# One order of steps for another in a kernel of gated attention and a feed-forward layer

## The chip, the cores and the metric

The kernel runs on one core of one Trainium2 chip. A core has five engines with a queue of instructions each: PE (TensorE, matrix products), ACT (ScalarE), DVE (VectorE), POOL (GpSimd) and SP (SyncE, which here issues nearly all DMA). The engines run beside each other and meet at semaphores. PE writes its products into PSUM, which has 8 banks; ACT and DVE read them from there. The metric is the time of one execution on the device in microseconds (us), lower is better; the median of three runs before the change is 181.44 us (180.72 to 181.81).

## The reference

Attention with a gated state runs over 4 batches, 8 heads, 768 positions and 48 numbers for each head; its output goes through a feed-forward layer with 384 inputs and 2048 inner units.

```python
f = 1.0 / (1.0 + np.exp(-f_logit))
for t in range(S):
    state = f[:, :, t, :, None] * state + np.einsum('bhd,bhe->bhde', k[:, :, t], v[:, :, t])
    y[:, :, t] = np.einsum('bhd,bhde->bhe', q[:, :, t], state)
x = y.transpose(0, 2, 1, 3).reshape(B * S, H * D)     # 3072 x 384
h = x @ w_in                                          # w_in 384 x 2048
g = h * np.cos(h)
out = g @ w_out                                       # w_out 2048 x 384
```

All inputs and the output are float32.

## The kernel before

The 3072 rows are cut into twelve pairs of 256 positions; pairs 0 to 2 belong to the first batch, and so on, and each pair needs the state that the pair before it in its batch left. The feed-forward layer works in twelve units of 256 rows, one for each pair. The function `describe` builds some 950 named steps, `pair(n)` those of attention and `moe(m, ...)` those of the layer. In a name, the first number is the pair, unit or row block, what follows the point is a part of it.

The steps of a pair are these, with the line of `kernel.py` on which the profile shows them:

- `f`, `k`, `q`, `v` load the inputs (L296); pairs 0 and 1 load f, k and q in halves of four heads.
- `ex`, `ln`, `fx`, `fy` on ACT make the logarithm of the gate, the gate and a factor (L329, L333, L347, L344); `ad` on POOL adds two logarithms (L363); `cum` on PE sums them over 64 positions (L374, L380); `eb` and `ei` on ACT turn the sums into decay factors (L391, L395).
- `qa` and `ka` lead q and k on (L338 or L341, and L351), `qm` and `km` multiply them with the decay factors (L404).
- `tq` and `tk` transpose the results, for pairs 0 to 3 on PE (L435, then `qkt` copies them out of PSUM), for pairs 4 to 11 `tq` is a DMA that SP issues (L424).
- `sc` on PE makes the scores (L455), `am` on DVE masks them (L459).
- `vb` and `vt` copy v into two layouts (L197, a helper for all copies).
- `ps` on PE makes the new part of the state (L477), `st` and `sz` on DVE add the old state and decay it (L495, L501).
- `y` and `yi` on PE give the output of attention (both L529), `xe` copies it out of PSUM (L197).

The steps of a unit are `h` (products with w_in, L577), `co` (a sine on ACT that gives the cosine, L582), `g` (the product h cos h on DVE, L559), `o` (products with w_out, L593), `ot` (copy out of PSUM, L197) and `out` (the store, L604). `w0`, `w1` load the two weight matrices in four parts each (L282) and `wc0`, `wc1` cast them to bfloat16 (L197). `zf` is a product of zeros into an unused bank (L264), `z...` with a tile's name sets a buffer to zero (L231).

Nothing in this program chooses the order at run time. The string `ORDER` lists all steps as `name:engine` with the letters T (PE), S (ACT), V (DVE), G (POOL), Y (SP), and with the number of the buffer or PSUM bank that a step's result gets. `emit` goes through it and issues each step on its engine, so that the string fixes the order of every queue; a buffer that is given out again makes the new writer wait for the last readers:

```python
    for word in ORDER.split():
        name, how = word.split(":")
        plan.append((G.steps[name], LETTER[how[0]], [int(x) for x in how[1:].split(",") if x]))
```

`SLOTS` says how many buffers there are of a kind (3 each for f, k, q, v, 5 for g, which weights on their way in use too). When ACT passes from the functions of the gate to the sine or back, it loads a table; both orders do so ten times.

Of the kernel before, what the change touches and what calls it, by code (L numbers as in the profile page):

```python
# [48 lines left out]
ei3:S1 k1.1:Y ka1.1:G ln2:S0 fy2:S km1.1:V ps1.0:T7,0 ad2:G1 vt1.1:G tq1.1:T6 zf43:T1 zf44:T1  # L49
zf45:T1 zf46:T1 tk1.1:T qkt1.1:S0 sz0.10:V qkt1.0:V2 ps1.1:T zf47:T1 sc1.0:T4 st1.00:V st1.01:V  # L50
xe0.1:S0 am1.0:V2 fx3:S cum2:T1 eb2:S2 xe0.0:V fx2:S ei2:S2 w0.0:Y1 wc0.0:G zf48:T6 zf49:T6 zf50:T6
zf51:T6 sc1.1:T4 am1.1:V0 h0.01:T2 h0.00:T sz1.00:V0 y1:T6,1 co0.0:S2 sz1.01:V st1.11:V yi1:T
xe1.0:S1 st1.10:V w0.1:Y0 wc0.1:G xe1.1:V sz1.10:V0 h0.11:T4 k3:Y2 ka3:G h0.10:T h1.01:T6 sz1.11:V
co0.1:S0 g0.0:V0 h1.00:T km3.1:G0 tk3.1:T0 co1.0:S3 g0.1:V q3:Y0 qa3:G qm3.1:G tq3.1:T qm3.0:G
h1.10:T2 km3.0:G w0.2:Y1 wc0.2:S w0.3:Y2 wc0.3:G h1.11:T co1.1:S1 qkt3.1:V3 sc3.1:T4 g1.0:V3
h1.20:T0 h1.21:T co1.2:S0 h0.31:T6 h0.30:T co0.3:S2 am3.1:V3 q2:Y1 qa2:G qm2.0:G2 w1.2:Y4 wc1.2:G
k2:Y2 h0.21:T4 g1.1:V h0.20:T co0.2:S3 tq3.0:T2 tk3.0:T g1.2:V g0.3:V h1.31:T0 h1.30:T co1.3:S1
tq2.0:T3 g0.2:V o3.2:T6 o2.2:T7 o0.2:T4 qm2.1:G ka2:G km2.0:G km2.1:G o1.2:T5 tk2.0:T qkt3.0:V1
w1.3:Y1 wc1.3:S g1.3:V o2.3:T o3.3:T sc3.0:T0 am3.0:V1 qkt2.0:S4 sc2.0:T2 am2.0:V2 w1.0:Y2 wc1.0:G
# [18 lines left out]
co4.3:S0 st6.10:V g4.3:V h4.21:T0 h4.20:T co4.2:S2 o6.0:T ot6:S3 h5.11:T2 h5.10:T co5.1:S3 h4.10:T4
g4.2:V st6.11:V sz6.11:V2 g5.1:V3 h4.11:T co4.1:S2 g4.1:V h5.20:T0 h5.21:T o9.3:T7 co5.2:S1 g5.2:V
sz6.10:V o9.0:T o8.0:T2 o8.3:T vb7:G0 qa6:G qm6.0:G qm6.1:G f8:Y1 tq6.1:Y4 sc6.1:T4 am6.1:V2  # L80
tq6.0:Y3 sc6.0:T0 ka7:G km7.0:G1 vt7.2:G2 vt6.0:G0 km7.1:G vt6.1:G qa7:G qm7.0:G vt7.0:G ps7.1:T6,3
ps7.0:T vt6.2:G vt7.1:G st7.00:V sz7.00:V1 st7.01:V sz7.01:V st7.11:V st7.10:V sz7.10:V0 v8:Y1
out2:Y out6:Y sz7.11:V out4:Y q9:Y1 tq7.0:Y2 ex9:S ln9:S1 ex8:S vt6.3:S qm7.1:G tq7.1:Y0 o8.2:T
o9.2:T o8.1:T ot8:V1 o7.1:T4 o9.1:T o7.3:T fy9:S ad9:G2 cum9:T5 ln8:S0 fy8:S am6.0:V0 o7.0:T o7.2:T
ot7:V0 ad8:G1 vt7.3:G cum8:T6 yi6:T3 qa9:G ot9:V3 fx9:S y6:T2 xe6.1:V1 fx8:S ei9:S2 eb9:S2 vb8:G0
k9:Y0 ka9:G km9.0:G2 q8:Y0 qa8:G vt8.2:G0 f10:Y0 k8:Y2 q10:Y2 sc7.0:T0 am7.0:V3 f11:Y2 out5:Y out8:Y
sc7.1:T4 am7.1:V1 eb8:S1 ei8:S1 v9:Y0 ka8:G km8.0:G0 vt8.1:G h5.00:T6 xe6.0:S qm8.0:G tq8.0:Y1
km9.1:G qm9.1:G vb9:G1 qm9.0:G km8.1:G h5.30:T2 h5.31:T co5.3:S3 g5.3:V h6.30:T0 h5.01:T co5.0:S0
g5.0:V h6.31:T out7:Y v10:Y1 out9:Y tq9.0:Y3 tq9.1:Y4 yi7:T4,5 y7:T xe7.1:V3 xe7.0:S co6.3:S3
g6.3:V1 h6.20:T2 h6.21:T co6.2:S2 g6.2:V h6.01:T6 h6.00:T co6.0:S1 h6.11:T4 h6.10:T co6.1:S0  # L90
h7.11:T0 h7.10:T h7.20:T2 h7.21:T g6.0:V o12.0:T7 g6.1:V o10.2:T5 o12.3:T co7.1:S3 o13.0:T6 g7.1:V0
co7.2:S2 g7.2:V sc8.0:T0 vt9.2:G1 qm8.1:G tq8.1:Y0 ps8.1:T4 ps9.0:T2,3 vt9.1:G ps9.1:T sz9.00:V1
ps8.0:T st8.00:V sz9.01:V st8.01:V sz8.01:V3 st9.11:V o13.2:T o10.1:T sz8.00:V o12.1:T st9.10:V
o13.3:T sz9.10:V2 ex11:S ln11:S1 ad11:G1 ex10:S vt9.3:G sz9.11:V ln10:S0 fx10:S cum11:T2 o12.2:T
ei11:S0 eb11:S1 o13.1:T ad10:G0 cum10:T3 vt9.0:S ot13:S2 ei10:S2 o11.1:T4 o11.0:T ot12:V1 am8.0:V3
# [620 lines left out]
```

## Time and profile before

| what | number |
|---|---|
| median of 3 runs | 181.44 us (180.72 to 181.81) |
| span of the profiled execution, first to last instruction | 178.2 us |
| what lies around the span, against that median | 3.2 us |
| PE busy, fill products among it | 170.5 us |
| DVE busy | 136.6 us |
| ACT busy | 127.2 us |
| POOL busy | 112.9 us |
| read from and written to memory | 25.17 MB and 4.72 MB |

The profile comes from one execution; no time of its own is listed for it beside its span. Times in its rows are counted from the start of the span. A row of a group gives the line, the engine, the operation, what it writes and reads, how often; behind the first bar the busy time in all and the mean of one in nanoseconds, behind the second the idle time of the engine just before these instructions and who ended it. A row of the timeline begins with start and length in microseconds. A row of the chain has start, length and what the last-ending chain of work did there.

### The profile page before, as it was taken

What the parts mean: (1) busy time and instruction counts of PE and PEld (TensorE: products, weight loads), DVE (VectorE), ACT (ScalarE), POOL (GpSimd) and SP (SyncE); (2) the same over time, 40 slices, a digit from 0 to 9 for tenths busy, and PEclk for the clock granted to TensorE, in tenths of its full rate; (3) what the DMA queues carried; (4) which work ended last, traced back from release to release, by engine and by line L of the source; (5) the groups of instructions that cost most, each with busy time, mean ns of one, the idle gap of its engine ahead of it and who ended that gap; (6) DMA issues with size and microseconds to landing.
All of it is one profiled execution on the core that took longest, in us unless ns stands there. A gap on an engine that the chain in (4) does not pass through costs nothing.

```text
span 178.2 us, 5848 instructions
## 1 busy us (share of the span) xinstructions
PE 170.5 (96%) x2475; PEld 122.8 (69%) x2478; DVE 136.6 (77%) x206; ACT 127.2 (71%) x179; POOL 112.9 (63%) x145
## 2 busy tenths in 40 slices
...
GB/s 148 261 261 264 307 221 362 328 359 277 293 258 258 222 241 232 289 166 188 246 198 274 255 198 238 178 287 143 2 59 169 144 48 4 0 88 4 0 177 88
DMA packets 74394, 34.46 MB, mean 193 GB/s; under 512 B 67456, under 2 KB 72832, under 8 KB 74368
## 3 DMA queue, kind: packets, MB, share of 16 engines
...
q8 instruction: 19, 0.31, 0.7%
...
HBM read 25.17 MB, written 4.72 MB: 168 GB/s over the span
## 4 chain that ended last, share of the span: by engine, by line
PE 84%; DVE 6%; SPq 4%; DMA 3%; issue 1%; ACT 1%; DVEq 0%
PE ps L593 36%; PE ps L577 35%; PE ps L529 5%; SPq L296 4%; PE ps L455 3%; DMA k<-in_k_dram 3%; DVE am L459 2%; PE ps L477 2%; DVE qk L404 1%; PE ps L435 1%; PE ps L374 1%; DVE ps L495 1%; ACT w_in_bf L197 1%; DVE x L197 1%; PE ps L264 0%
## 5 line engine op out<-in xcount | busy, mean ns | idle before, releaser
L559 DVE TENSOR_TENSOR g<-ps,co 128x1024 bf16<-128x1024 f32 x48 | 58.0, 1222 | 20.0 <-ACT co L582 17.1
L582 ACT ACTIVATE co<-ps,halfpi 128x1024 bf16<-128x1024 f32 x48 | 53.0, 1114 | 24.5 <-PE ps L577 21.4
L593 PE MATMUL ps<-w_out_bf,g 128*128 128x384 bf16 x384 | 68.0, 326 | 0.0
L577 PE MATMUL ps<-x,w_in_bf 128*128 128x256 bf16 x576 | 66.9, 273 | 0.4 <-ACT w_in_bf L197 0.3
L577 PEld LDWEIGHTS <-w_in_bf 128*128 128x128 bf16 x576 | 55.5, 98 | 9.0 <-ACT w_in_bf L197 0.5
L593 PEld LDWEIGHTS <-g 128*128 128x128 bf16 x384 | 36.2, 98 | 21.5
L459 DVE TENSOR_TENSOR am<-ps,pmask 128x1024 bf16<-128x1024 f32 x24 | 28.8, 1219 | 4.3 <-PE ps L455 4.0
L197 POOL COPY vt<-vb 64x384 bf16<-64x384 bf16 x40 | 20.6, 516 | 3.1 <-ACT vb L197 1.3
L404 POOL TENSOR_TENSOR qk<-q,b 128x384 bf16<-128x384 f32 x21 | 20.9, 1002 | 2.0 <-DVE q L338 1.3
L404 POOL TENSOR_TENSOR qk<-k,bi 128x384 bf16<-128x384 f32 x20 | 19.9, 1001 | 0.7
L264 PE MATMUL ps<-zero 128*128 128x512 bf16 x49 | 14.8, 426 | 1.5 <-DVE zero L203 1.2
L501 DVE TENSOR_TENSOR sz<-ps,b 64x192 bf16<-64x192 f32 x40 | 14.1, 352 | 2.4 <-PE ps L477 1.6
L351 POOL TENSOR_TENSOR k<-k,f 128x384 f32<-128x384 f32 (+1 forms) x13 | 11.8, 909 | 6.0 <-DMA k<-in_k_dram 3.5
L197 ACT COPY ot<-ps 128x384 f32<-128x384 f32 (+1 forms) x15 | 6.6, 456 | 9.6 <-PE ps L593 5.0
L495 DVE TENSOR_TENSOR ps<-ps,sz 64x192 f32<-64x192 f32 x32 | 11.7, 365 | 1.8 <-PE ps L477 0.8
L329 ACT ACTIVATE f<-f 128x768 f32<-128x768 f32 (+1 forms) x14 | 10.4, 744 | 3.3 <-DMA f<-in_f_logit_dram 2.6
L363 POOL TENSOR_TENSOR sp<-ls 128x384 bf16<-128x384 f32 x10 | 10.1, 1007 | 4.0 <-ACT ls L333 3.8
L341 POOL TENSOR_TENSOR q<-f,q 128x384 f32<-128x384 f32 x10 | 10.0, 998 | 3.9 <-ACT f L344 2.8
L197 POOL CAST vb<-v 128x768 bf16<-128x768 f32 x10 | 8.6, 856 | 1.5 <-DMA v<-in_v_dram 1.5
L455 PEld LDWEIGHTS <-qkt 48*64 48x64 bf16 x384 | 6.2, 106 | 4.5 <-issue 2.4
L455 PE MATMUL ps<-qkt 48*64 48x128 bf16 x384 | 8.8, 220 | 0.5 <-DVE am L459 0.2
L264 PEld LDWEIGHTS <-zero 128*128 128x128 bf16 x52 | 4.8, 105 | 5.7 <-issue 1.9
...
## 6 DMA issues: line engine op xcount, KB each, us to landing
...
```

The lines of the kernel that those rows point to most:

```text
L197: (nc.scalar.copy if e == "ACT" else eng(e).tensor_copy)(out=o, in_=i)
L264: G.step(f"zf{i}", ("PE",), lambda e, dump=dump: nc.tensor.matmul(dump.ap, lhsT=zero[:, 0:128], rhs=zero, start=True, stop=True), writes=[ ...
L351: eng(e).tensor_mul(out=w.ap[:, :, 0, :], in0=w.ap[:, :, 0, :], in1=t.ap[:, :, 0, :])
L404: G.step(f"{nm}{n}.{u}", ("POOL", "DVE") if cut else ("POOL",), lambda e, u=u, j=j, src=src, dec=dec: eng(e).tensor_mul(out=qkp[u][j].ap[: ...
L455: nc.tensor.matmul(o[64 * h:64 * h + 64, r, 2 * a + g, :].rearrange("p (e n) -> p e n", e=2), lhsT=qkv(u)[s, 1, a, g, h, :], rhs=qkv(u)[s, ...
L459: G.step(f"am{n}.{u}", ("DVE",), lambda e, u=u, sc=sc: nc.vector.tensor_mul(out=am[u].ap.rearrange("p r b n -> p (r b) n"), in0=sc.ap.rear ...
L495: nc.vector.tensor_add(out=view()[s], in0=view()[s], in1=S0.ap[s, :, r, :])
L501: eng(e).tensor_mul(out=new.ap[s, :, r, :].rearrange("p (u a) n -> p u a n", u=2), in0=view()[s].rearrange("p (u a) n -> p u a n", u=2), i ...
L559: nc.vector.tensor_mul(out=o.rearrange("p b (n e) -> p b n e", e=2), in0=ph.ap.rearrange("p (b e n) -> p b n e", e=2, n=64), in1=co.ap.rea ...
L577: nc.tensor.matmul(ph.ap[:, i * T:(i + 1) * T].rearrange("p (g t) -> p g t", t=C), lhsT=w_in_bf[:, kk, f0:f0 + 128], rhs=xa[:, :, kk, :], ...
L582: G.step(f"co{m}.{j}", ("ACT",), lambda e, ph=ph, co=co: nc.scalar.activation(out=co.ap, in_=ph.ap, func=AF.Sin, bias=halfpi), reads=[ph], ...
L593: nc.tensor.matmul(po.ap[:, 0:DM], lhsT=gT.ap[:, j, i * C:(i + 1) * C], rhs=w_out_bf[:, j, :], start=(po.first and j == 4 * s), stop=(po.f ...
```

## The change

`ORDER` is replaced as a whole: 928 steps instead of 947. The work is the same except for 19 of the 52 fill products, which are gone. The order of every queue is new, and so are most buffers and banks. Among the loads, `v0` comes second and `k0`, `q0` before `f1`; `f6` and `v6` come behind the DMA transposes of pairs 4 and 5, where they were ahead of them. Some steps change engine: `km0.0`, `km0.1` and `km1.1` go from DVE to POOL, `qm0.1` from DVE to POOL and `qm1.1` from POOL to DVE, twelve more of the 48 `vt` copies from POOL to ACT (20 instead of 8), three casts of w_out instead of one and no cast of w_in on ACT (`wc0.2` on POOL), `vb2` and `vb3` from ACT to POOL and `vb10` the other way, `qkt0.0` to DVE and `qkt3.1` to ACT, eleven `ot` (`ot23.0` among them, to ACT) and seven `xe` one way or the other between ACT and DVE, `ka0.1` to DVE. On PE the products with the weights stand between clusters of attention's short products in both orders, in other places.

```diff
--- before.py
+++ after.py
...
 WITHIN = 12
-ZEROS = 52
+ZEROS = 33
...
 ORDER = """
-f0.1:Y0 zqk.1:G zsp.1:G zvt.0:G zsz.0:V zsp.2:V zsp.0:V zqk.0:G zvt.2:G zsz.3:G f0.0:S zsz.2:V
-ex0.1:S ln0.1:S1 fx0.1:S zf0:T0 zf1:T0 zf2:T0 zf3:T0 zf4:T0 zf5:T0 zf6:T0 zf7:T0 zf8:T0 cum0.1:T7
-ei0.1:S2 ex0.0:S f1.1:Y1 k0.1:Y0 ln0.0:S fx0.0:S ex1.1:S zf9:T6 zf10:T6 zf11:T6 zf12:T6 cum0.0:T0
-ka0.1:G km0.1:V1 zvt.1:V zf13:T1 tk0.1:T3 v0:Y2 ei0.0:S eb0.0:S2 q0.1:Y0 eb0.1:S qa0.1:V qm0.1:V
-zf14:T2 zf15:T2 zf16:T2 zf17:T2 zf18:T2 zf19:T2 zf20:T2 zf21:T2 tq0.1:T vb0:G1 k0.0:Y ka0.0:G
-vt0.1:G1 zsz.1:G vt0.2:G km0.0:V zf22:T2 zf23:T2 zf24:T2 zf25:T2 zf26:T2 tk0.0:T4 qkt0.1:V1 zqk.2:V
-f1.0:Y ex1.0:S ln1.0:S1 ln1.1:S fx1.1:S ps0.0:T2,5 ps0.1:T sz0.00:V1 f3:Y2 ex3:S q0.0:Y qa0.0:V
-fx1.0:S sz0.01:V vt0.3:G ln3:S1 ad3:G0 k1.0:Y2 ka1.0:V cum1.1:T1 ei1.1:S0 v1:Y1 st0.11:V qm0.0:V
-eb1.1:S0 fy3:S st0.10:V vb1:G0 vt1.2:G0 cum1.0:T7 ei1.0:S sz0.11:V3 zf27:T6 zf28:T6 zf29:T6 sc0.1:T2
-am0.1:V3 q1.1:Y1 qa1.1:V qm1.1:G0 zf30:T6 zf31:T6 zf32:T6 zf33:T6 tq0.0:T qkt0.0:S4 zf34:T6 cum3:T6
-zf35:T0 zf36:T0 sc0.0:T0 vt1.3:S f2:Y0 km1.0:V zf37:T4 zf38:T4 zf39:T4 tk1.0:T4 am0.0:V1 q1.0:Y
-eb3:S1 vt0.0:S zf40:T2 zf41:T2 zf42:T2 y0:T2,3 yi0:T qa1.0:V eb1.0:S qm1.0:V tq1.0:T vt1.0:G ex2:S
...
-vt3.0:G vt2.3:G k5:Y0 f6:Y1 v4:Y2 ps3.0:T1,2 ps3.1:T sz3.00:V2 ps2.0:T3 ps2.1:T vt2.1:G o0.0:T
-st2.00:V sz3.01:V q5:Y0 v5:Y1 o1.3:T o1.0:T ad4:G0 sz2.00:V1 st3.10:V sz3.10:V3 sc2.1:T0 ad5:G2
-st2.01:V sz2.01:V am2.1:V0 o2.1:T o3.1:T fx5:S ot2:V1 ot3:V0 st3.11:V o0.1:T qa4:G yi2:T0,3 y2:T
-xe2.0:V1 xe2.1:V yi3:T1 y3:T7 cum4:T6 ei4:S1 ka4:G sz3.11:V eb4:S0 qm4.1:G0 o1.1:T ot1:V2 ot0:V3
-km4.0:G qm4.0:G v6:Y0 tq4.0:Y3 ka5:G km4.1:G tq4.1:Y2 cum5:T0 eb5:S2 ei5:S0 xe3.0:V3 h2.11:T2
-h2.10:T co2.1:S0 vb4:G2 xe3.1:V h2.20:T4 g2.1:V1 h2.01:T6 h2.00:T co2.0:S2 g2.0:V f7:Y0 vt4.2:G0
-fy5:S out1:Y out3:Y vt4.0:G qa5:G qm5.0:G1 km5.0:G tq5.0:Y1 km5.1:G qm5.1:G tq5.1:Y0 vb5:G0 h3.10:T0
...
-y4:T6,0 yi4:T xe4.0:V2 ps5.1:T1 ps5.0:T st5.00:V sc5.1:T4 am5.1:V2 fx7:S vt5.0:G vb6:G1 vt5.2:G
-vt5.1:G ka6:G sc5.0:T2 am5.0:V0 cum7:T6 o6.1:T o6.2:T xe4.1:S h4.01:T4 eb7:S0 ei7:S0 h4.00:T
-co4.0:S0 h3.01:T2 st5.01:V sz5.01:V2 y5:T0,6 sz5.00:V yi5:T xe5.1:S0 fy6:S g4.0:V0 h3.00:T xe5.0:V
...
-o21.3:T ot21:S2 o22.1:T4 o22.3:T ot20:S1 out20:Y out16:Y g11.2:V o22.2:T g11.0:V o22.0:T ot22.1:S1
-out22.1:S o23.0:T7 o23.1:T ot22.0:V o23.3:T o23.2:T ot23.0:V3 out22.0:S ot23.1:S out14:Y out21:Y
-out23.1:Y out23.0:S
+zsp.1:G zvt.0:G f0.0:S2 f0.1:Y ex0.0:S ln0.0:S1 zvt.2:G v0:Y0 ex0.1:S ln0.1:S zf0:T7 zf1:T7 zf2:T7
+zf3:T7 zf4:T7 zf5:T7 zf6:T7 zf7:T7 zf8:T7 cum0.0:T0 zqk.0:V zsz.0:V fx0.0:S zvt.1:V ei0.0:S1 vb0:G1
+vt0.2:S1 k0.0:Y1 ka0.0:G k0.1:Y fx0.1:S q0.0:Y1 qa0.0:V q0.1:Y f1.0:Y0 km0.0:G0 zf9:T7 zf10:T7
+cum0.1:T3 eb0.1:S2 ei0.1:S f1.1:Y ka0.1:V eb0.0:S qm0.0:V ex1.0:S ln1.0:S1 q1.1:Y0 ex1.1:S ln1.1:S
+k1.1:Y2 fx1.1:S qa0.1:V km0.1:G zf11:T7 zf12:T7 zf13:T7 zf14:T7 zf15:T7 zf16:T7 zf17:T7 ps0.0:T5,4
+f2:Y1 tk0.0:T6 zsz.3:G tq0.0:T qkt0.0:V3 qm0.1:G vt0.0:S vt0.1:G k1.0:Y zf18:T0 zf19:T0 tk0.1:T1
+sc0.0:T2 am0.0:V3 f3:Y2 cum1.0:T6 qa1.1:V ka1.1:G zf20:T0 cum1.1:T7 eb1.1:S1 tq0.1:T v1:Y1 qkt0.1:V2
+q1.0:Y ps0.1:T zf21:T2 zf22:T2 sc0.1:T2 ei1.1:S0 ei1.0:S qm1.1:V0 ex2:S ln2:S1 sz0.01:V3 sz0.00:V
+st0.11:V am0.1:V1 km1.1:G fx1.0:S vt0.3:G eb1.0:S st0.10:V w0.0:Y3 sz0.10:V0 ad2:G1 tq1.1:T1 zf23:T0
+tk1.1:T vb1:G0 zf24:T0 zf25:T0 zf26:T0 yi0:T2 vt1.3:G0 ka1.0:V vt1.0:G qkt1.1:S0 y0:T5 w0.1:Y4
+km1.0:V cum2:T6 xe0.1:S1 sz0.11:V zf27:T0 zf28:T0 zf29:T0 zf30:T0 ps1.1:T7,1 qa1.0:V q3:Y1 sc1.1:T2
+qm1.0:V zf31:T0 tq1.0:T4 am1.1:V3 ex3:S ps1.0:T eb2:S0 tk1.0:T qkt1.0:V4 ln3:S0 ad3:G1 fx3:S cum3:T0
+zf32:T2 sc1.0:T2 w0.2:Y0 vt1.2:S wc0.0:G xe0.0:S st1.01:V sz1.01:V3 h0.00:T4 zqk.2:V vt1.1:S wc0.1:G
+h0.01:T fx2:S am1.0:V1 fy3:S y1:T3,2 k3:Y1 st1.00:V sz1.00:V st1.10:V yi1:T ei2:S0 eb3:S2 st1.11:V
+qa3:G xe1.1:V0 h0.10:T6 xe1.0:V w0.3:Y1 ei3:S2 co0.0:S2 h0.11:T h1.11:T2 h1.10:T co0.1:S1 g0.0:V4
+q2:Y0 qm3.1:G2 wc0.2:G ka3:G h1.00:T4 w1.0:Y0 k2:Y2 h1.01:T g0.1:V co1.1:S0 km3.1:G wc0.3:G h1.20:T6
...
+tk2.1:T6 o1.2:T qm2.1:G tq2.1:T f5:Y0 ex5:S ln5:S1 o0.2:T w1.1:Y0 qkt2.1:V0 wc1.3:G v2:Y2 fx5:S
+sc2.0:T4 ad5:G1 wc1.1:S am2.0:V1 sc2.1:T6 am2.1:V2 o3.2:T f4:Y2 o3.3:T o1.3:T o2.2:T o0.3:T cum5:T6
+o2.3:T sc3.0:T4 am3.0:V3 ei5:S1 vb2:G0 v3:Y1 fy5:S q4:Y1 eb5:S1 k4:Y2 vt2.1:G1 ps2.1:T7 ps2.0:T
+vt2.2:G ex4:S o1.1:T ln4:S0 v4:Y2 o3.1:T ot3:S1 vt2.0:G vt2.3:G vb3:G2 st2.01:V ad4:G1 st2.00:V
+o2.1:T sz2.01:V3 fy4:S sz2.00:V y2:T4,5 yi2:T xe2.0:V0 vt3.1:G1 xe2.1:V ps3.1:T0,7 ps3.0:T sz3.00:V0
+sz3.01:V st3.11:V ot2:S3 fx4:S qa4:G out3:Y q5:Y2 o0.1:T ot1:S2 k5:Y0 vt3.3:G ka4:G st3.10:V cum4:T6
+h2.21:T4 sz3.11:V3 v5:Y1 vt3.0:S vt3.2:S h2.20:T sz3.10:V f7:Y1 ei4:S2 eb4:S0 qm4.0:G0 ot0:V0 yi3:T0
+y3:T3 co2.2:S0 xe3.1:V1 vb4:G1 vt4.3:G2 h2.11:T6 xe3.0:V h2.10:T km4.0:G tq4.0:Y1 h3.10:T2 h3.11:T
+co2.1:S3 g2.2:V1 h3.21:T0 h3.20:T qm4.1:G h2.01:T4 vt4.0:S co3.1:S0 h2.00:T km4.1:G tq4.1:Y4 ka5:G
+km5.1:G2 f6:Y2 co3.2:S2 g2.1:V vt4.2:S km5.0:G h2.30:T6 g3.1:V4 zsz.1:V h2.31:T out2:Y k6:Y0
+co2.0:S0 g3.2:V h3.31:T2 g2.0:V co2.3:S1 h3.30:T vt4.1:S o5.2:T0 co3.3:S2 o5.0:T ex7:S o4.0:T1 qa5:G
+ln7:S1 qm5.0:G tq5.0:Y2 g2.3:V qm5.1:G tq5.1:Y0 o5.1:T sc4.0:T4 g3.3:V sc4.1:T2 ps4.1:T6,7 ps4.0:T
+o5.3:T o4.1:T ot5:S1 o4.2:T zsz.2:G v6:Y2 ex6:S ln6:S0 am4.0:V1 st4.00:V st4.01:V sz4.00:V1 sz4.01:V
+o4.3:T ot4:S3 ad7:G1 cum7:T6 yi4:T5,4 v7:Y0 q6:Y1 vb5:G2 vt5.1:G0 fx6:S am4.1:V2 y4:T st4.11:V
+o6.3:T0 sc5.1:T2 eb7:S2 ad6:G1 sz4.11:V0 st4.10:V out1:Y ps5.1:T1 q7:Y0 ka6:G zqk.1:V vt5.3:G vb6:G1
+xe4.0:V3 ps5.0:T xe4.1:S sz4.10:V zsp.2:V am5.1:V0 sc5.0:T4 cum6:T7 vt5.0:S o6.2:T vt5.2:G vt6.1:G2
+st5.00:V st5.01:V o6.1:T ei7:S0 eb6:S0 ei6:S2 km6.0:G0 am5.0:V2 sz5.01:V2 h4.01:T2 h4.00:T km6.1:G
+sz5.00:V fx7:S co4.0:S3 h3.00:T6 fy6:S qa6:G y5:T4,1 g4.0:V2 out4:Y k7:Y2 yi5:T xe5.0:V2 out0:Y
+qm6.1:G xe5.1:S qm6.0:G h3.01:T ps6.0:T5,1 ps6.1:T fy7:S sz6.01:V1 h4.20:T2 sz6.00:V h4.21:T qa7:G
...
+o20.3:T g10.0:V co11.0:S3 g11.0:V o21.2:T o22.3:T4 o22.0:T co11.1:S0 out18:Y g11.1:V o20.0:T o20.2:T
+ot20:S3 o22.1:T o23.2:T5 out17:Y o21.0:T o22.2:T ot22.0:V0 ot22.1:S out20:Y out22.1:Y o23.1:T
+ot21:S1 o23.0:T o23.3:T ot23.1:S2 out22.0:Y out21:Y out23.1:Y ot23.0:S out23.0:S zsp.0:V
 """
```

More of the change, by code (lines that the diff above doesn't have):

```diff
@@ L48 @@
-eb3:S1 vt0.0:S zf40:T2 zf41:T2 zf42:T2 y0:T2,3 yi0:T qa1.0:V eb1.0:S qm1.0:V tq1.0:T vt1.0:G ex2:S
[L49 to L59, printed above, removed]
@@ L78 @@
[L78 to L89, printed above, removed]
@@ L90 @@
[L90 to L95, printed above, removed]
```

65 lines of the change are left out of this document (39 added, 26 removed).

## The prediction

> **What bounds the kernel now.** I read the page first, then busy time by stage, then the chain that ended last in order of time, then groups by form, and the timeline only where the chain leaves TensorE.
>
> ```profile
> span 178.2 us, 5848 instructions
> PE 170.5 (96%) x2475; PEld 122.8 (69%) x2478; DVE 136.6 (77%) x206; ACT 127.2 (71%) x179; POOL 112.9 (63%) x145
> ```
>
> The span is 178.2 us; the three runs have a median of 181.44, so 3.2 us lie around the span, and I add them unchanged at the end. The 96% is not yet a bound: fill products of zeros (L264) count as busy. The stages tell the difference.
>
> ```profile
> 5.14:25.19 20.05, 17.25 (x279) 9.72 (x281) 15.96 (x29) 15.56 (x35) 13.72 (x17) 1.00 1.08 262
> 25.19:32.85 7.66, 7.27 (x128) 6.00 (x129) 7.38 (x12) 6.52 (x8) 7.09 (x7) 1.00 1.06 341
> 32.85:53.98 21.13, 21.13 (x344) 15.31 (x345) 17.86 (x27) 17.14 (x21) 16.91 (x20) 1.00 1.16 299
> 53.98:77.45 23.47, 23.39 (x394) 17.93 (x396) 20.31 (x29) 21.92 (x31) 21.58 (x27) 1.00 1.14 248
> 77.45:121.50 44.05, 44.05 (x733) 32.97 (x734) 38.62 (x55) 36.94 (x52) 36.65 (x45) 1.00 0.98 216
> 121.50:175.00 53.50, 53.46 (x604) 39.49 (x600) 32.85 (x40) 26.50 (x33) 13.20 (x18) 1.00 0.29 72
> ```
>
> Columns: stage, its length, then busy time and instructions of PE, PEld, DVE, ACT, POOL, clock, DMA share, GB/s. From 32.85 us to the end PE misses 0.1 us in 142: whatever the order, this work can only be kept full or spoiled. In 53.98 to 77.45 ACT is at 21.92 of 23.47 and POOL at 21.58: little room. The time that can be won lies before 32.85 us, as the chain shows.
>
> ```profile
> 23.36 1.23 DVE am L459
> 24.58 0.48 DVE x L197
> 25.06 0.14 issue
> 25.19 1.47 PE ps L577 x12
> ...
> 31.34 1.47 ACT w_in_bf L197
> 32.85 4.10 PE ps L577 x36
> ```
>
> The first product with weights (h0) starts at 25.19, behind VectorE's mask `am1.0` and the cast `xe0.0`; a cast of weights (`wc0.2`, on ScalarE) stops PE once more until 32.85.
>
> **The change part by part.**
>
> *Same work, other cover.* No step is added or lost but 19 of 52 fill products. PE still changes between long and short products as often (58 stretches of short steps before, 56 after, counted in the order), so the interleaving itself I price at nothing: 36 products of L577 take 4.10 us (0.11 each) however they are cut, 12 take 1.47 with their tail.
>
> *The fill products.* 49 of them show:
>
> ```profile
> L264 PE MATMUL ps<-zero 128*128 128x512 bf16 x49 | 14.8, 426 | 1.5 <-DVE zero L203 1.2 <-issue 0.2
> 1.19:5.14 3.95, 3.95 (x9) 1.19 (x9) 1.00 0.88 210
> 5.56:6.60 1.04, 1.04 (x4) 0.31 (x4) 1.00 1.29 265
> ```
>
> The last two rows are windows of L264 alone: 0.44 us each at first, 0.26 later. Nineteen at 0.26 are at most 4.9 us of PE, all where PE waits for others; alone they are worth 0. What they cover is told with the rivals.
>
> *Loads.* The loads that SP issues ahead of `w0.0` are the same ones in another order. Their users show the landings:
>
> ```profile
> 7.45 0.82 POOL L197 CAST vb<-v 128x768 bf16<-128x768 f32 x1 [0.80 <-DMA v<-in_v_dram]
> 8.25 0.36 DVE L338 SCALAR_TENSOR_TENSOR q<-f,q 128x192 f32<-128x192 f32 x1 [0.73 <-DMA q<-in_q_dram]
> 9.68 0.52 ACT L329 ACTIVATE f<-f 128x384 f32<-128x384 f32 x1 [1.17 <-DMA f<-in_f_logit_dram]
> ```
>
> In the old order these are the whole `v0`, then the halves `q0.1` and, two halves on, `f1.0`: 0.7 to 0.8 us for each half. Counting halves, `q0.0` takes the seventh place that `q0.1` had (8.2 us), and `f1.0` keeps the ninth (9.7). DVE's chain to the first attention output (`y0`) thus starts when it did, and only what it carries counts.
>
> *VectorE to y0.* Before `y0` DVE loses two `km` and one each of `sz`, `st` and a zeroing, and gains a `qkt` copy.
>
> ```profile
> L404 DVE TENSOR_TENSOR qk<-k,bi 128x384 bf16<-128x384 f32 x4 | 3.0, 754 | 2.3 <-POOL k L351 2.3
> L197 DVE COPY qkt<-ps 128x1024 bf16<-128x1024 bf16 x5 | 3.4, 682 | 0.4 <-PE ps L435 0.4
> L501 DVE TENSOR_TENSOR sz<-ps,b 64x192 bf16<-64x192 f32 x40 | 14.1, 352 | 2.4 <-PE ps L477 1.6
> 18.80 0.63 PE L529 MATMUL ps<-am,vt 128*32 128x128 bf16 x32
> ```
>
> 2 x 0.75 + 2 x 0.35 (`st` taken like `sz`) + 0.25 for the zeroing - 0.68 = 1.8 us less. Against it stand two waits that the chain gets instead, for `tq0.0` before `qkt0.0` and for `sc0.0` before `am0.0`, some 0.2 us each. `y0` moves from 18.8 to 17.4. The `km` go to POOL, beside DVE's remaining `qm`; that can cost, as these rows show:
>
> ```profile
> 8.71 0.56 DVE L404 TENSOR_TENSOR qk<-q,b 128x384 bf16<-128x384 f32 x1
> ...
> 13.43 0.99 POOL L363 TENSOR_TENSOR sp<-ls 128x384 bf16<-128x384 f32 x1 [1.28 <-ACT ls L333]
> 13.58 1.25 DVE L404 TENSOR_TENSOR qk<-q,b 128x384 bf16<-128x384 f32 x1
> ```
>
> One form takes 0.56 us, or 1.25 when POOL had begun a two-operand instruction. New order: `qm0.0` meets `km0.1` and `qm1.1` meets `km1.1`, so 0 to 2 x 0.69 us; I take 0.3, because the mean above (0.75) already holds such meetings.
>
> The Trainium skill, "SBUF — State Buffer", section "Who interferes with whom", says that VectorE with two SBUF inputs and GpSimd reading SBUF hold one port in turn, for whole instructions. By it the 1.25 us case comes at both places and the sum would be 1.1 us worse; the two rows agree with the rule.
>
> *ScalarE to the first sine.* After `y0` (17.7 + 0.6) ACT has thirteen instructions before its table load: `xe0.1`, `ex3`, `eb2`, `ln3`, `fx3`, `vt1.2`, `xe0.0`, `vt1.1`, `fx2`, `fy3`, `ei2`, `eb3`, `ei3`.
>
> ```profile
> L329 ACT ACTIVATE f<-f 128x768 f32<-128x768 f32 x10 | 8.3, 834 | 0.6 <-POOL w_out_bf L197 0.6
> L344 ACT ACTIVATE f<-f 128x384 f32<-128x384 f32 x10 | 5.1, 522 | 0.1
> L197 ACT COPY vt<-vb 64x384 bf16<-64x384 bf16 x8 | 4.1, 507 | 0.1
> 58.74 4.27 ACT L582 ACTIVATE co<-ps,halfpi 128x1024 bf16<-128x1024 f32 x4
> 25.32 1.28 ACT L582 ACT_TABLE_LOAD   x1
> ```
>
> Two at 0.84 and eleven near 0.5 are 7.2 us, less 5% since neighbours overlap (four sines of 1.11 in 4.27): 6.8. The load starts at 25.1 instead of 25.32. `h0` needs less: `xe0.0` (the seventh, 22.1) and `wc0.0`, which POOL does after `ad3` (`ln3` done at 20.8, +1.0, +1.46 = 23.3). So PE starts h0 at 23.3, 1.9 us earlier; the sines only 0.2.
>
> *Units 0 and 1.* Old: table load 25.32 to the end of the eighth sine.
>
> ```profile
> 38.75 1.11 ACT L582 ACTIVATE co<-ps,halfpi 128x1024 bf16<-128x1024 f32 x1 [0.59 <-PE ps L577]
> ...
> ACT co L582 <- PE ps L577: 1.9, 4, 0.8
> ACT co L582 <- ACT co L582: 0.6, 1, 0.6
> ```
>
> The last two rows are ACT's waits within it: 14.5 us, 2.5 of them waiting. New, ACT has 8 x 1.05 + table 1.28 + `fy2` 0.5 + `qkt3.1` 1.0 + `wc1.0` 1.46 (a weight cast as in the chain, 1.47) = 12.6; PE is ahead of it by 1.7 us more, so I leave 0.6 for waits: 25.1 + 13.2 = 38.3 against 39.86, 1.6 earlier. `wc0.2` leaves ACT for POOL, and the stop before 32.85 with it. Next late would be g0 to g1: VectorE has one mask and two `sz` between them, as before.
>
> *Pairs 2 to 5.* Twelve `vt` copies move from POOL to ACT over the whole kernel. From the eighth sine to the cast `xe5.1` ACT's list sums to 35.4 us in the old order and 38.7 in the new (three more `vt`, three `ot`, one weight cast, one `fy`, two `vb` fewer, all from rows like those above).
>
> ```profile
> 76.74 0.48 ACT L197 CAST x<-ps 128x384 bf16<-128x384 f32 x1 [0.45 <-PE ps L529]
> 77.38 0.44 PE L477 MATMUL ps<-vb,qk 64*64 64x48 bf16 x32
> ```
>
> The old list took 37.35 us (39.86 to 77.21): 33.6 after overlap and 3.7 of waits. New: 36.7 and waits between 0 and 3.7. Waits shrink when ACT becomes the later of two; I take 1.1, nearer to nothing. `xe5.1` ends at 38.3 + 36.7 + 1.1 = 76.1 instead of 77.21. It frees a PSUM bank for `ps6.0`, which is PE's next stop: 76.2 for 77.38, 1.2 us earlier. PE by itself would be there at 77.38 - 1.9 = 75.5, so ACT sets it.
>
> *The rest.* From `ps6.0` on both orders hold the same PE work; ACT's surplus shrinks there and VectorE falls behind nowhere by count: 0, bounds -0.3 to +1.0. The tail changes `ot23.0` from DVE to ACT; both halves of that row were already copied one behind the other, so 0, bounds 0.3 each way.
>
> **Sum.** -1.2 us on the profiled 178.2, and on the median: 181.44 - 1.2 = 180.2.
>
> **The rivals.** *All of the start is kept* (1.9 us): ACT finds no waits at all in pairs 2 to 5, `xe5.1` ends at 75.0, PE binds. 181.44 - 1.9 = 179.5. For it: PE full after 32.85. Against: ACT at 93% there.
>
> *ACT eats it.* With all 3.7 us of waits `xe5.1` ends at 78.7, +1.5 at most; half way, 76.9, gives 181.1. For it: old waits came from PE, POOL and DMA, and only those for PE must shrink. No measurable difference.
>
> *Slower: a load behind a transpose.* SP now issues `v6` after the transpose `tq5.1`, which waits for POOL's `qm5.1`; before, `v6` stood ahead of `tq4.0`.
>
> ```profile
> 64.18 3.15 SPq L424 DMA_TRANSPOSE qkt<-qk  x2
> DMA to landing us min/median/max: 4.3/5.6/8.6
> 75.72 0.63 PE L529 MATMUL ps<-am,vt 128*32 128x128 bf16 x32
> ```
>
> The first row is `tq5`, the second the landing of v, the third `y5`. Issued at 67.3 as now, `v6` lands at 72.9 or, at worst, 75.9; `vb6` (0.82) and `vt5.2` (0.5), which `y5` needs, follow on POOL: 74.2 or 77.2. It decides from a landing of 7.1 us on, when `y5` is later than 75.7; `km6` and the transposes of pair 6 and 7 follow in POOL's order, so at worst +1.5, and 0.5 for the next pair: 183.4.
>
> *Slower clock.* The rows of the fill products show PE at half pace in its first 4 us. If fewer fills let that return before h0, the first 24 products of 0.11 us take twice as long: +2.6 at most, 182.8. The Trainium skill, "TensorE: Matmul & The Clock Gate", section "HAM oscillation — how this bites in real kernels", asks for no idle gap over about 3.4 us; the largest gap that I count in the new start is near 1.5, so by that rule it does not happen, and no row here tests it.
>
> **How the numbers follow.** Forecast (180.2) 0.30 and the start kept 0.20 make faster 0.50. ACT eats it: 0.23, same. Load behind a transpose 0.20, clock 0.03, and other waits that a full PE has no room for 0.04: slower 0.27. Half a per cent, 0.9 us, is about what a measurement tells from no change; 180.2 stands barely beyond it. The range goes from 178.6 (start kept, 1.9; no meeting on VectorE, 0.3; the rest and the tail at their lower bounds, 0.6) to 183.2, into the late load. Faster cases alone: 178.6 to 180.5.
>
> **What would show it.** h0 near 23.3 and `y0` near 17.7; the eighth sine ending near 38.3; PE without gaps after that but for small ones before `ps6.0`; the last product 1.2 us before 175.0. Wrong, if the first group of L577 starts no earlier than 25.19, if DVE's `qk` on line 404 has a mean above 1.0 us, or if PE waits in 40 to 80 us for `vt`, `am` or a transpose.

## The result, and the profile after

The changed kernel takes 182.61 us (median of 18 runs, 180.48 to 184.77), the kernel before 181.48 us (18 runs, 180.05 to 182.60). The ratio is 1.0055, with a 95% interval from 1.0029 to 1.0081: slower by about half a per cent, where 180.2 us and a gain were forecast. Measured again beside the first experiments the changed kernel gave 182.52 us and 1.002 [0.998, 1.006], which by itself is no difference. The ratios leave out executions more than 1.5% above the fastest of their kernel, among them two at a granted clock of 0.564 (289.34 us of the kernel before, 283.05 us of the last kernel below).

One thing first, since every number below depends on it. The time of each execution now stands beside its span, and the two differ by 1.8 us in all of them (182.31 and 180.5 for the profile below, 180.48 and 178.7 for the shortest run). By that, the span of 178.2 us, on which the prediction's sum was made, belongs to an execution of about 180.0 us, shorter than any of the 18 listed (from 180.05). The prediction put the whole 3.2 us up to the median outside the span. Only 1.8 of that lies there; the other 1.4 us lie inside the span of a median execution, and a second profile of the old kernel, below, shows two waits of that kind.

The first lines of the page of the changed kernel, and its busy time by stage with the columns of the prediction (stage, length, then PE, PEld, DVE, ACT and POOL, clock, DMA share, GB/s):

```profile
span 180.5 us, 5811 instructions
PE 169.6 (94%) x2459; PEld 121.9 (68%) x2459; DVE 135.2 (75%) x206; ACT 132.7 (74%) x191; POOL 107.1 (59%) x133
```

```profile
23.28:32.85 9.57, 9.40 (x134) 8.02 (x135) 8.98 (x14) 8.23 (x11) 9.21 (x8) 1.00 1.07 322
53.98:77.45 23.47, 23.30 (x412) 17.75 (x410) 21.20 (x34) 21.89 (x31) 20.81 (x26) 1.00 1.08 233
77.45:121.50 44.05, 42.55 (x638) 31.45 (x638) 37.12 (x51) 36.08 (x50) 31.21 (x38) 1.00 0.98 207
121.50:175.00 53.50, 53.03 (x663) 39.45 (x652) 34.45 (x43) 27.74 (x34) 12.82 (x16) 1.00 0.25 69
```

Between 77.45 and 121.50 us TensorE lacks 1.50 us of 44.05. In the first profile of before it lacked none there. The chain that ended last shows the largest stop, 1.02 us (start and length in us):

```profile
104.80 1.12 ACT co L579
...
105.95 2.37 DVE g L556 x2
108.31 0.39 SPq L601
...
108.76 5.12 DMA out_dram<-ot
...
113.96 0.56 DVE ot L194
114.52 2.27 DVE am L456 x2
...
116.84 0.37 PE ps L474 x13
```

In the timeline the same place reads, on VectorE and then on TensorE:

```profile
113.96 0.56 DVE L194 COPY ot<-ps 128x384 f32<-128x384 f32 x1 [1.70 <-DMA out_dram<-ot]
```

```profile
116.84 0.37 PE L474 MATMUL ps<-vb,qk 64*64 64x48 bf16 x13 [1.02 <-DVE am L456]
```

VectorE's copy `ot10` needs slot 1 of `ot`, which the store `out8` is still reading. Two masks stand behind it, and TensorE's `ps8.0` behind those. `out8` went out late because of SyncE's queue:

```profile
102.76 1.23 SPq L421 DMA_TRANSPOSE qkt<-qk  x1
104.04 0.58 SPq L293 DMA_DIRECT2D v<-in_v_dram  x1
104.72 0.58 SPq L601 DMA_DIRECT2D out_dram<-ot  x1
105.76 1.47 SPq L421 DMA_TRANSPOSE qkt<-qk  x1
107.33 0.53 SPq L293 DMA_DIRECT2D f<-in_f_logit_dram  x1
107.95 1.23 SPq L601 DMA_DIRECT2D out_dram<-ot  x2
```

The first row is the transpose `tq8.0`, which waits for GpSimd's product `qm8.0` (done at 102.74 us). `out8` is the second of the two stores in the last row. Its tile was filled at 90.6 us, but five other issues stand between that transpose and it, one of them `tq9.0`, which waits for GpSimd in its turn (until 105.73 us). The chain above names VectorE's `g` ahead of the store because it ended just then; the store needs only its tile.

A second profile of the changed kernel was an execution of 180.67 us (span 178.9) without this wait. Its rows for VectorE's `ot10` and for `tq8.0`:

```profile
112.34 0.56 DVE L194 COPY ot<-ps 128x384 f32<-128x384 f32 x1 [0.33 <-PE ps L590]
...
101.56 1.23 SPq L421 DMA_TRANSPOSE qkt<-qk  x1
```

Here the queue ran 1.2 us earlier, because GpSimd had begun `qa9` (line 338), which needs the load `q9`, at 95.51 us instead of 96.71. The row of the first profile:

```profile
96.71 1.00 POOL L338 TENSOR_TENSOR q<-f,q 128x384 f32<-128x384 f32 x1 [1.38 <-ACT x L194]
```

The row names ScalarE as the releaser, but the trace has `q9` landing at 96.58 us here and at 95.39 in the second profile, 0.13 and 0.12 us before `qa9` begins, so it is the load. The times of the changed kernel fall into two groups: in the second measurement four of twelve between 180.54 and 180.67 us, the rest from 182.39 upward (of the first eighteen, one at 180.48 and one at 181.79, the rest from 182.19). Each group has one profile.

The landmarks of the prediction, in us, with the two profiles of each kernel:

| landmark | before, 1st | before, 2nd | forecast | after, 1st | after, 2nd |
|---|---|---|---|---|---|
| first h0 | 25.19 | 25.09 | 23.3 | 23.28 | 23.36 |
| `ps6.0` | 77.38 | 77.28 | 76.2 | 76.40 | 76.50 |
| last product begins | 174.63 | 177.12 | 173.4 | 176.67 | 175.06 |
| from `ps6.0` to there | 97.25 | 99.84 | 97.2 | 100.27 | 98.56 |

Up to `ps6.0` the two profiles of a kernel agree within 0.1 us. What lies behind it differs from one execution to the next, by 2.6 us in the old kernel and 1.7 us in the new.

### The profile page after: what moved, and what is told of

Its sections match the earlier page's. It is cut to its first block, busy times and chain, and to the rows that moved or that the text cites. A ratio compares the mean times of both kernels' runs of the same rounds, so it can differ in the third digit from the quotient of the medians.

```text
span 180.5 us, 5811 instructions
## 1 busy us (share of the span) xinstructions
PE 169.6 (94%) x2459; PEld 121.9 (68%) x2459; DVE 135.2 (75%) x206; ACT 132.7 (74%) x191; POOL 107.1 (59%) x133
## 4 chain that ended last, share of the span: by engine, by line
PE 70%; DVE 11%; ACT 7%; DMA 5%; SPq 2%; issue 2%; DVEq 0%
PE ps L574 33%; PE ps L590 27%; PE ps L526 4%; DVE am L456 4%; DMA out_dram<-ot 3%; PE ps L452 3%; DMA f<-in_f_logit_dram 3%; SPq L293 2%; DVE ps L492 1%; DVE sz L498 1%; DVE g L556 1%; ACT co L579 1%; PE ps L474 1%; ACT f L326 1%; PE ps L432 1%
## 5 line engine op out<-in xcount | busy, mean ns | idle before, releaser
L574 PE MATMUL ps<-x,w_in_bf 128*128 128x256 bf16 x576 | 67.7, 273 | 0.5 <-POOL w_in_bf L194 0.4
L401 POOL TENSOR_TENSOR qk<-k,bi 128x384 bf16<-128x384 f32 x23 | 23.0, 1010 | 1.8 <-ACT b L388 0.6
L194 POOL COPY vt<-vb 64x384 bf16<-64x384 bf16 x28 | 14.5, 518 | 1.3
L194 POOL CAST vb<-v 128x768 bf16<-128x768 f32 x11 | 9.1, 827 | 7.2 <-DMA v<-in_v_dram 7.1
L348 POOL TENSOR_TENSOR k<-k,f 128x384 f32<-128x384 f32 (+1 forms) x12 | 11.2, 934 | 2.8 <-ACT f L344 2.5
L261 PE MATMUL ps<-zero 128*128 128x512 bf16 x33 | 11.2, 461 | 1.2 <-DVE zero L200 1.2
L194 DVE COPY ot<-ps 128x384 f32<-128x384 f32 (+1 forms) x10 | 5.3, 533 | 9.0 <-PE ps L590 7.1
L194 ACT COPY vt<-vb 64x384 bf16<-64x384 bf16 x20 | 10.1, 508 | 1.0 <-POOL vb L194 0.8
```

What stands on the lines that cost most here:

```text
L194: (nc.scalar.copy if e == "ACT" else eng(e).tensor_copy)(out=o, in_=i)
L261: G.step(f"zf{i}", ("PE",), lambda e, dump=dump: nc.tensor.matmul(dump.ap, lhsT=zero[:, 0:128], rhs=zero, start=True, stop=True), writes=[ ...
L401: G.step(f"{nm}{n}.{u}", ("POOL", "DVE") if cut else ("POOL",), lambda e, u=u, j=j, src=src, dec=dec: eng(e).tensor_mul(out=qkp[u][j].ap[: ...
L574: nc.tensor.matmul(ph.ap[:, i * T:(i + 1) * T].rearrange("p (g t) -> p g t", t=C), lhsT=w_in_bf[:, kk, f0:f0 + 128], rhs=xa[:, :, kk, :], ...
```

## The experiments

**The changed kernel again.** This run is the measure for the next three.

> The changed kernel once more, as the measure for the runs beside it. Expected 1.003 to 1.008 of the kernel before, with the wait of VectorE for the store of the output tile (line 194, some 1.7 us near 112 us) in its profile again.

Measured: 182.52 us, 1.002 [0.998, 1.006], beside 182.00 us for the kernel before. The profiled execution is the second one above, without the wait. Both parts of the expectation missed.

**The stores moved ahead.** SyncE's order alone:

```diff
-tq8.0:Y2 v9:Y1 ... out6:Y ... tq9.0:Y0 f10:Y2 ... out7:Y ... out8:Y
+out6:Y out7:Y out8:Y tq8.0:Y2 v9:Y1 ... tq9.0:Y0 f10:Y2
```

> The three stores out6, out7 and out8 are moved ahead of the transpose tq8.0 in SyncE's order; nothing else changes. Theory (out8 stands in SyncE's queue behind transposes and loads that wait, so that its slot of `ot` comes free late and VectorE, then TensorE, stop near 112 to 117 us): the wait of 1.70 us for the store is gone, TensorE's stop before ps8.0 (1.02 us) and part of those behind it go too, and the time falls by 1.0 to 1.8 us against the changed kernel, to 0.996 to 1.000 of the kernel before. Rival (the late transposes of pair 8 and 9 set that place in any case): the wait goes, the time falls by at most 0.3 us, 1.003 or more.

Measured: 180.67 us, 0.994 [0.991, 0.997], 1.85 us below the changed kernel. VectorE no longer waits for the store:

```profile
112.47 0.56 DVE L194 COPY ot<-ps 128x384 f32<-128x384 f32 x1 [0.34 <-PE ps L590]
```

Three stores in another place of one queue turn the loss into a gain. `tq8.0` goes out at 102.78 us here, as late as in the first profile, so late transposes alone do not make the loss. From `ps6.0` (76.31) to the last product (175.20) this profile takes 98.89 us, against 100.27 in the first.

**One slot more.** SyncE's order stays; only the slot of `ot10` changes.

```diff
-SLOTS = {... "ot": 4}
+SLOTS = {... "ot": 5}
-ot10:V1
+ot10:V4
```

> `ot` gets a fifth slot, and ot10 is written there instead of into the slot that out8 still stores; SyncE's order stays as it is. Theory of the late store: the same gain as with the stores moved ahead, 1.0 to 1.8 us, 0.996 to 1.000 of the kernel before, though out7 and out8 still go out at 108 to 109 us. Rival (the queue delays the transposes themselves, and these set the place): no change, 1.003 to 1.008.

Measured: 181.27 us, 0.998 [0.995, 1.001], 1.25 us below the changed kernel. The stores still go out at 108.24 us, later than in the first profile, and the copy does not wait for them. So the shared slot is worth about 1.25 us of the 1.85. For the other 0.6 us the queue remains: in this profile TensorE stopped for 0.68 us at 110.59, before `ps9.1`. That it is all of the rest isn't shown.

**One load moved ahead.**

```diff
-tq8.0:Y2 v9:Y1
+v9:Y1 tq8.0:Y2
```

> The load v9 alone is moved ahead of the transpose tq8.0 in SyncE's order. By the theory of the late store, GpSimd's wait of 1.36 us for v9 (line 194) goes, VectorE's wait for the store of `ot` stays, and the time falls by 0 to 0.5 us, 1.000 to 1.008 of the kernel before. By the rival (GpSimd is late by v9, so km9.1 and the transposes tq9.1 and tq8.1 are late, and these set the place) the gain is the larger one here: 1.0 us or more, 1.000 or less.

Measured: 181.20 us, 0.998 [0.994, 1.002], 1.3 us below the changed kernel: the rival's size, not mine. The profile has neither GpSimd's wait for `v9` nor VectorE's for the store (112.16 us, 0.34 us for TensorE). But in this execution `qa9` began at 95.66 us, early as in the second profile, so the missing wait for the store proves nothing here. Taking one issue out from behind `tq8.0` brings the stores forward too. The run doesn't separate the two reasons; the fifth slot, which leaves SyncE's order as it is, speaks for the store.

**Two loads moved ahead of two transposes.**

```diff
-tq7.0:Y0 tq7.1:Y1 f11:Y1 q8:Y1 q9:Y0
+q8:Y1 q9:Y0 tq7.0:Y0 tq7.1:Y1 f11:Y1
```

> The loads q8 and q9 are moved ahead of the transposes tq7.0 and tq7.1 in SyncE's order; all stores stay where the change put them, out8 behind tq8.0 and tq9.0 too. The single runs of the changed kernel fall into two groups, 180.5 to 180.7 and 182.2 to 183.1 us. Theory (q9, issued behind two transposes, lands near 95.5 or near 96.7 us; GpSimd's masks, the transpose tq8.0 and with it out8 follow 1.2 us later in the second case, and only then does VectorE wait for out8's slot): GpSimd no longer waits near 96 us, tq8.0 goes out at 101.5 us or sooner, the upper group is gone, and the median is 180.5 to 181.0 us, 0.992 to 0.997 of the kernel before. Rival (the store itself takes longer in some runs): both groups stay, median 182 us or more.

Measured: 184.26 us, 1.015 [1.010, 1.020]. GpSimd did `qa8` and `qa9` one behind the other, from 93.09 us on and without a wait, so it was the loads that they had waited for; the stop near 116 us is gone.

```profile
93.09 1.95 POOL L338 TENSOR_TENSOR q<-f,q 128x384 f32<-128x384 f32 x2
```

But TensorE now stands still for 2.15 us up to 92.30, for the transposes that had been moved back by two issues (first row below), and then the granted clock falls (third number from the end):

```profile
92.30 0.42 PE L452 MATMUL ps<-qkt 48*64 48x128 bf16 x16 [2.15 <-DMA qkt<-qk]
```

```profile
93.00:96.00 3.00, 2.76 (x27) 1.54 (x28) 2.90 (x5) 1.26 (x3) 2.53 (x4) 0.50 1.06 254
```

The other five of the six executions, at a mean clock of 0.988 to 0.990, took 183.94 to 184.54 us; the one at 0.997 took 182.85. My expectation failed: it reckoned with what the loads gain and not with what stands behind them.

**The old kernel again.**

> The kernel before once more, for a second profile. All later runs show 1.8 us between span and time, and the span of the first profile, 178.2, would then be a run of 180.0, where the median is 181.5: that profile showed one of the fastest runs. If so, this one has, with 5 chances in 6, a span of 179.2 to 180.6 and a stop of TensorE of 1 to 2 us that the first had not; the theory names no place for it. If the first profile was typical, the span is 178.2 within 0.3 and the time outside it 3.2.

Measured: 182.48 us, span 180.7. TensorE has two stops that the first profile had not:

```profile
101.65 6.06 DMA v<-in_v_dram
107.77 0.82 POOL vb L197
108.59 1.92 POOL qk L404 x2
110.56 0.69 PE ps L477 x44
...
134.76 5.27 DMA qkt<-qk
140.08 0.42 PE ps L455 x16
```

```profile
140.08 0.42 PE L455 MATMUL ps<-qkt 48*64 48x128 bf16 x16 [1.59 <-DMA qkt<-qk]
```

A load that took 6.06 us to land made GpSimd's order 0.7 to 0.8 us late. Behind it went out the transposes of pairs 10 and 11, also 0.8 us late, and the one that TensorE waited for took 5.27 us to land where the first profile has 3.44. So the old order, too, has little reserve against slow transfers behind 100 us. Its first profile showed a case in which all of them were in time. The span is 0.1 us above the range that was expected; a stop of the expected size came.

**Zeroings off VectorE.** On top of the moved stores:

```diff
-... zsz.1:V ... zqk.1:V ... zsp.2:V ...
+zqk.1:G zsp.2:G zsz.1:G vb0:G1
```

> On top of the moved stores out6 to out8: the zeroings zqk.1, zsp.2 and zsz.1 go from VectorE (59 to 71 us) to GpSimd's idle time before 6 us. Theory (VectorE, not ScalarE, sets pairs 2 to 5): TensorE's stops near 68.6 (for am4.1) and 70.7 us (0.18 us of idleness for a cast x) shrink, ps6.0 comes 0.3 to 0.6 us earlier than the 76.2 of the kernel with the moved stores alone, and the time is 0.2 to 0.6 us below that kernel's 180.67. Rival (ScalarE sets it, as predicted): ps6.0 stays, no change beyond 0.1 us.

Measured: 180.50 us, 0.996 [0.993, 0.999]; `ps6.0` at 76.21 against 76.31. The idleness before the scores at 70.7 us is gone, but that was worth 0.1 us (0.2 counted from h0, which came 0.1 later in this profile), the rival's size. These three zeroings on VectorE cost next to nothing; which engine sets the stage they do not show.

**Copies between ScalarE and GpSimd, both ways.** On top of the moved stores, six copies that the change gave to ScalarE go back:

```diff
-vt3.0:S vt3.2:S vt4.0:S vt4.2:S vt4.1:S vt5.0:S
+vt3.0:G vt3.2:G vt4.0:G vt4.2:G vt4.1:G vt5.0:G
```

> On top of the moved stores out6 to out8: six of the copies that the change gave to ScalarE (vt3.0, vt3.2, vt4.0, vt4.1, vt4.2, vt5.0) go back to GpSimd. If ScalarE sets pairs 2 to 5, as predicted, 3.0 us fewer there let xe5.1 end 0.6 us earlier, until TensorE binds: ps6.0 near 75.6 and the time 0.6 us below the 180.67 of the kernel with the moved stores alone. If VectorE sets it: ps6.0 stays at 76.2 or comes later, because GpSimd has 3.0 us more before its masks; 0 to +1.0 us.

Measured: 184.54 us, 1.018 [1.013, 1.024]; `ps6.0` at 79.17, beyond both expectations. The waits of TensorE's weight loads now show GpSimd as the one that is late (sum, count, longest):

```profile
PEld L526 <- POOL vt L194: 2.4, 4, 1.2
PEld L452 <- DMA qkt<-qk: 2.1, 3, 1.1
PEld L474 <- POOL qk L401: 2.1, 4, 0.7
```

The other way, on top of the moved stores and zeroings:

```diff
-vt3.1:G1 vt3.3:G vt5.1:G0
+vt3.1:S1 vt3.3:S vt5.1:S0
```

> On top of the moved stores and the zeroings on GpSimd: three more copies of pairs 3 and 5 (vt3.1, vt3.3, vt5.1) go from GpSimd to ScalarE. If ScalarE sets pairs 2 to 5, as predicted, its 1.5 us more make xe5.1 and ps6.0 1.0 to 1.5 us later (76.1 becomes 77.1 or more) and the time 1.0 to 1.5 us longer than 180.5. If GpSimd is the engine without room there (six copies given back cost 4 us), ScalarE has 2.1 us of idleness between 38.0 and 76.1 us to take them: ps6.0 within 0.4 of 76.1, the time 180.2 to 180.8.

Measured: 181.58 us, 0.998 [0.996, 1.001]. That is 1.1 us above the kernel without it by the medians, but the two were measured on two occasions, with the kernel before at 182.12 and 181.45 us; by the ratios it is 0.5 us. `ps6.0` moves from 76.21 to 77.28.

Three copies of 0.5 us move that landmark by 1.07 us, as expected if ScalarE has no room there. Six copies the other way cost about 4 us, because GpSimd is then late. Both engines have little room in this stage (21.89 and 20.81 us busy of 23.47 in the changed kernel). That ScalarE set the place in the changed kernel itself does not follow from this.

**Without most fill products.** On top of the moved stores and zeroings:

```diff
-ZEROS = 33
+ZEROS = 9
-zf9:T7 ... zf32:T2
```

> On top of the moved stores and the zeroings on GpSimd: of the 33 fill products the last 24 (zf9 to zf32, between 7 and 23 us) are left out. They compute nothing that is used. A stop of 2.15 us of TensorE at 92 us was followed by 3.3 us at a granted clock of 0.50 in an earlier run, stops of 1.02 and 1.6 us were not. By that, the start without fills has the clock at 0.50 for most of 9 to 23 us and for up to 3.4 us after h0.00: the first products with weights take up to twice as long, h1.20 comes 1.5 to 2.5 us later, and the time is 181.8 to 183.2 us. Rival (only a wholly idle stretch of 3.4 us brings the clock down, and the longest gap stays below that): clock 1.00, time 180.2 to 180.8.

Measured: 183.01 us, 1.005 [1.002, 1.008], 2.5 us above the kernel with its fills by the medians (measured on two occasions; 1.7 us by the ratios). The clock by stage, and the first group of h0:

```profile
8.00:10.00 2.00, 1.09 (x24) 0.78 (x24) 1.64 (x4) 0.83 (x4) 1.38 (x2) 0.83 1.28 261
10.00:29.00 19.00, 14.68 (x275) 10.69 (x274) 16.15 (x28) 15.06 (x29) 15.07 (x18) 0.50 1.17 316
30.00:34.00 4.00, 4.00 (x39) 3.58 (x38) 3.08 (x3) 2.93 (x3) 3.23 (x3) 1.00 1.02 291
```

```profile
24.30 2.74 PE L573 MATMUL ps<-x,w_in_bf 128*128 128x256 bf16 x12
```

h0 begins 1.0 us later than with the fills (24.30 against 23.30), twelve products take 2.74 us instead of 1.48, and the clock comes back only five microseconds after h0. In this profile `ps6.0` comes 3.0 us later (79.20 against 76.21). The 33 fills that the change keeps are thus enough, and these 24 of them are worth 1.7 to 3 us. How much of that is the clock is shown for this execution (183.49 us, mean clock 0.944) alone: three of the ten list a mean clock of 1.00 and still took 182.25 to 182.48 us. What the clock did at their start is not known; the first fills of the kernel before ran at half pace where its clock, too, is given as 1.00.

**All moves together.** On top of the moved stores and zeroings:

```diff
-tq7.0:Y0 tq7.1:Y1 f11:Y1 q8:Y1 q9:Y0 ... tq8.0:Y2 v9:Y1
+tq7.0:Y0 tq7.1:Y1 q8:Y1 q9:Y0 f11:Y1 ... v9:Y1 tq8.0:Y2
```

> On top of the moved stores and the zeroings on GpSimd: the load v9 stands ahead of the transpose tq8.0, and the load f11 behind q8 and q9, so that q9 goes out one issue (0.58 us) sooner without holding back a transpose. Theory (from 86 us on SyncE's order sets the small stops): GpSimd does not wait for v9, ps9.1 no longer stops near 110 us (0.2 to 0.7 us), the runs lie closer together; median 180.0 to 180.4 us, 0.990 to 0.996 of the kernel before. Rival (what is left is set by VectorE): no more than 0.1 us against the 180.5 without the two moves.

> The kernel with all moves once more (stores out6 to out8 and load v9 ahead of the transpose tq8.0, load f11 behind q8 and q9, three zeroings on GpSimd), for a profile in the usual state and a second measurement. If the first result stands: 179.9 to 180.4 us, 0.987 to 0.994 of the kernel before; no stop of GpSimd for v9 near 108 us, none of VectorE for a store, and no stop of TensorE above 0.2 us before ps9.1; q9's mask qa9 starts at 95.0 to 95.6 us.

Measured: 180.14 us, 0.990 [0.985, 0.994], and again 180.05 us, 0.994 [0.991, 0.997]. This is faster than both kernels: the kernel before beside them had 182.12 and 181.39 us, 2.0 and 1.3 us more, and the changed one, on other occasions, 182.61 and 182.52. GpSimd passes from one cast of v to the next without waiting, and VectorE's copy waits for TensorE alone:

```profile
105.67 0.82 POOL L195 CAST vb<-v 128x768 bf16<-128x768 f32 x1
...
112.08 0.56 DVE L195 COPY ot<-ps 128x384 f32<-128x384 f32 x1 [0.34 <-PE ps L591]
```

One number missed its expectation: `qa9` was to start at 95.0 to 95.6 us. It starts at 94.28, and GpSimd then waits 0.92 us at 98.25 for a load of k, the next in the queue.

## Why the prediction was wrong, step by step

**VectorE to y0: right in effect.** `yi0` begins at 17.05 us, forecast 17.7 for the pair. The price for meetings with GpSimd was too low, though. I took 0.3 us:

```profile
9.38 1.15 DVE L335 SCALAR_TENSOR_TENSOR q<-f,q 128x192 f32<-128x192 f32 x1
...
13.66 0.91 DVE L401 TENSOR_TENSOR qk<-q,b 128x384 bf16<-128x384 f32 x1
```

The first takes 0.41 us elsewhere and began after a GpSimd instruction of 1.20 us (9.12), the second 0.54 and began after one at 13.16: 1.1 us together, 0.8 more than I took. Both rows agree with the rule of the Trainium skill, "SBUF — State Buffer", section "Who interferes with whom", that such instructions of the two engines contend; by it the prediction counted two meetings of 0.69 us, 1.4 us, one of them at another place. `yi0` still came 0.65 us early, so the rest of the chain was some 1.4 us shorter than I counted. Two errors cancelled, and the landmark came out by luck.

**ScalarE, units 0 and 1: right.** h0 at 23.28 (forecast 23.3), behind GpSimd's cast of w_in as forecast; the eighth sine's end at 38.14 (38.3).

**Pairs 2 to 5: the landmark right, the reason not.** `xe5.1` ends at 76.25 (forecast 76.1), `ps6.0` begins at 76.40 (76.2). But ScalarE was busy for 35.84 us of this stretch and idle for 2.27, where the sum had 36.7 and 1.1; the two errors nearly cancel. And `ps6.0` did not wait for ScalarE, as the rows show: TensorE goes from the product before to `ps6.0` without a stop.

```profile
75.64 0.83 PE L574 MATMUL ps<-x,w_in_bf 128*128 128x256 bf16 x6
76.40 0.44 PE L474 MATMUL ps<-vb,qk 64*64 64x48 bf16 x32
```

"PE by itself would be there at 77.38 - 1.9 = 75.5, so ACT sets it" took TensorE's pace from h0 on as unchanged. The same products take it 53.12 us from h0 to `ps6.0`, 52.19 before. By the distance between the starts of neighbouring products, small stops at 24.84, 25.62, 27.47, 33.29, 49.85, 64.59, 68.68 and 70.76 us cost 1.1 to 1.3 us, and each of them ends with a step of VectorE. What makes VectorE late at each of them was not tested. That GpSimd has as little room as ScalarE I had not priced.

**The rest: wrong, and this term decides.** "From `ps6.0` on both orders hold the same PE work; ACT's surplus shrinks there and VectorE falls behind nowhere by count: 0, bounds -0.3 to +1.0." Against the first profile of before it measured +3.02 us in one execution (100.27 against 97.25) and +1.31 in the other (98.56); by the medians it is about +2.1 (1.13 us slower, with 0.98 gained up to `ps6.0`). The count of the work was right, but counting work by engine can't see a queue: SyncE's order was compared for the start and for `v6`, not between 85 and 116 us. There the change put `out6`, `out8` and `v9` behind `tq8.0` and `q9` behind `tq7.0`, all of which had stood ahead of them. The 3.02 us are in two parts:

- 1.7 us that come and go (100.27 less 98.56). The stop before `ps8.0`, behind the store, is about 1.1 of it (1.35 us between the starts of neighbouring products, 0.26 where nothing waits); another 0.35 is the stop before `ps9.1`, for which GpSimd, itself late by `q9`, is late; the remaining 0.3 was not traced. Moving three stores took 1.85 us off the median.
- 1.3 us that stay: mostly small stops that the first profile of before had not. The row below is one; `y6` waits for the copy `ot7`.

```profile
95.51 0.63 PE L526 MATMUL ps<-am,vt 128*32 128x128 bf16 x32 [0.19 <-DVE ot L194]
```

The idle time is 0.19 us, but the group before it began 0.81 us earlier (94.70) and takes 0.45 to the next where nothing waits (24.84 to 25.29), so the stop costs 0.36. Two more stand before `y9` (for `sz`, at 120.6 us in the second profile) and at 135.2 us; by the distance between the starts of neighbouring products the three cost 1.1 us there.

**The base: also wrong.** The sum subtracted 1.2 us from an execution that was one of the old kernel's shortest, and added 3.2 us around its span where later runs have 1.8. The old kernel's second profile has 2.6 us more behind `ps6.0`. With both kernels at their shortest the change loses 0.4 us (180.48 against 180.05); which waits come and go decides the rest, and one profile of each can't tell. What makes a transfer land late in one execution and not in the next stays open.

**The rivals.** "A load behind a transpose" was the right kind at the wrong place. `v6` behind `tq5.1` did no harm: `y5` is not among TensorE's waits. It was a store behind `tq8.0`, which in the prediction's list falls under "other waits that a full PE has no room for", with a chance of 0.04. "Slower clock" did not happen: the clock is 1.00 in all stages above. "ACT eats it" and "all of the start is kept" fell with `xe5.1` (78.7 or 76.9, and 75.0, against 76.25).
